# Six buffers for blocks of x in place of two, with room from the q/k loads and from v, and another order of the last layers

## The chip, the core and the metric

One core of a Trainium2 chip runs the whole program. The metric is the device time of one execution in microseconds (us); lower is better.

Engines are named as in the profile: PE (TensorE, matrix products; PEld its weight loads), DVE (VectorE), ACT (ScalarE), POOL (GpSimd) and SP (SyncE, which issues nearly all DMAs here). Each takes its own instructions in the order written and stands still when the next one waits.

## What is computed

Attention with the 32 largest scores of each row, and behind it a two-layer network on its output.

```python
# q, k, v: (B, H, S, D) = (8, 8, 576, 64)
scores = matmul(q, k.transpose(0, 1, 3, 2)) / sqrt(D)
kth = np.partition(scores, -32, axis=-1)[..., -32:-31]
scores = np.where(scores >= kth, scores, -1e9)
attn = softmax(scores)
x = matmul(attn, v).transpose(0, 2, 1, 3).reshape(4608, 512)
h = x @ w_in                                  # (4608, 2048)
out = (h / (1 + exp(-1.702 * h))) @ w_out     # (4608, 512)
```

## The kernel before, in words

**Slots.** The attention is cut into 144 slots, 18 in each of the 8 batches. A slot holds 128 rows of scores for the two heads of a pair (there are four pairs, `hp` 0 to 3). Of the 576 rows of a batch, four blocks `t` of 128 give 16 slots; the 64 rows left over go, for two pairs at once, into 2 slots, which stand ahead of the last block's four (line 262 on). So a batch's slots are t=0 (four pairs), t=1, t=2, two end slots, t=3.

**Iterations.** Slots 0 to 11 run one by one (`slot`, L754) while the weights come in. From slot 12 on `two_slots(n)` (L836) handles slots n and n+1, n even; one call is called an iteration here. In it DVE finds the largest of slots n and n+1; ACT masks, exponentiates and splits slots n-1 and n into 16-bit halves (`split`, L457), which SP writes to memory (`rows`) and brings back transposed (`turn_by_dma`, L465, tile `pt`, two buffers); PE multiplies slots n-3 and n-2 by v (`values_at`, L517); ACT copies the products (L902); and POOL scales them into x (`x_of`, L535, L544). PE also makes the scores of slots ahead (L281), and two steps of each layer.

**x and the layers.** A block of x, transposed, is a tile `xT` of 128 x 4 x 128 numbers, filled by the four pairs of one t. The 64 rows left over of two batches share a tile `xT_t`. When the last pair is in, `finish_x` (L549) appends the block to the list `ready`. `hidden` (L566) takes the oldest block on that list and makes a quarter of its first layer (16 products, L575) in PSUM tile `ph`. `tanh` (L587, ACT) and `gate` (L599, POOL's L604 and L605, or DVE's L607 in the end) turn that into `th`, and `project` (L612, four products, L622) adds it to the second layer's `po`. Each iteration calls `hidden` twice and `project` twice, so a block takes two iterations in each layer. In 36 slots (two batches) nine blocks become ready, at an uneven pace: the block of the ends comes in the odd batch just ahead of t=3, so that around the change from an odd batch to the next two blocks wait while the next are being filled.

```python
    loads = pool("loads", 2)      # q and k of a pair, as loaded
    vals = pool("vals", 6)        # v of a pair
    xtp = pool("xtp", 2)          # blocks of x
```

**Loads.** A table says in which slot, counted from a batch's first, the steps for the pairs are written into the program (L651 to L655, L670 on): FETCH loads q and k of a pair (`load`, L171: six DMAs into one tile `qk_l`), READY makes halves of it on ACT (`prepare_by_dma`, L234, tile `halves`), writes these to memory (`qk_rows`, four DMAs) and brings them back transposed (`turn`, L250, tile `qk_t`), and VALUES loads v (`load_v`, L195: three DMAs). The names with `_1` are for batch 1, which comes while the weights still arrive. SP thus issues, in one order, loads of q, k and v, `qk_rows`, `qk_t`, `rows`, `pt` and the output. It stands still ahead of a DMA whose source isn't written or whose target isn't free.

**The end.** After slot 143 the loop goes on without attention, and `last_slot` (L828) works off what is left:

```python
    def last_slot():
        tanh(False)
        gate(False)
        if may_project(0):
            project(range(G))
        hidden()
```

Of the kernel before, what the change touches and what calls it, by code (L numbers as in the profile page):

```python
# [9 lines left out]
ALU = mybir.AluOpType  # L10
ENG = mybir.EngineType
F32 = mybir.dt.float32
# [6 lines left out]
P = 128  # L19
# [11 lines left out]
def kernel(  # L31
# [27 lines left out]
    nc = tc.nc  # L59
# [11 lines left out]
    G = 4  # L71
# [17 lines left out]
    const = ctx.enter_context(tc.tile_pool(name="const", bufs=1))  # L89
    pool = lambda name, bufs, **kw: ctx.enter_context(tc.tile_pool(name=name, bufs=bufs, **kw))  # L90
    raws = pool("raws", 8)
    loads = pool("loads", 2)
    vals = pool("vals", 6)
    qkt = pool("qkt", 6)
    scp = pool("scp", 4)
    prp = pool("prp", 2)
    lefts = pool("lefts", 2)
    small = pool("small", 4)
    ptp = pool("ptp", 2)
    xtp = pool("xtp", 2)  # L100
    xtt = pool("xtt", 1)
    thp = pool("thp", 5)
    apart = pool("apart", 4, space=DRAM)
# [54 lines left out]

    qT, kT, vv = {}, {}, {}
    loaded = {}  # L160
    v_ends = [const.tile([P, 2, D], F32, name=f"v_e{i}") for i in range(6)]
    for i, t in enumerate(v_ends):
        (nc.gpsimd if i else nc.vector).memset(t[:], 0.0)

# [6 lines left out]
    def load(name, b, hp, queue=None):  # L171

        src = q if name == "q" else k
        if (b, hp) not in loaded:
            loaded[b, hp] = loads.tile([P, 2 * NF + 1, 2, D], F32, name="qk_l")
        t = loaded[b, hp]
        if queue is None:
            heads_of = lambda j: of_load(name, t)[:, :, j, :]
        else:
            heads_of = lambda j: heads_apart(name, t)[:, j, :, :]  # L180
        queue = queue or nc.sync
        for j in range(2):
            queue.dma_start(heads_of(j), src[b, 2 * hp + j, 0:FULL, :].rearrange("(p t) d -> p t d", t=NF))

        on = slice(0, TAIL) if name == "q" else slice(TAIL, P)
        queue.dma_start(t[on, 2 * NF, :, :], src[b, 2 * hp : 2 * hp + 2, FULL:S, :].rearrange("h p d -> p h d"))
# [283 lines left out]

    xts = {}

    def values(n, put_off=None):

        b, t, hps = slots[n]
        pt = st[n]["pt"]
        outs = []
        for p in range(2 if t == NF else 1):
            cols = slice(p * TAIL, (p + 1) * TAIL) if t == NF else slice(0, P)
            main, tail = vv[b, hps[p]]  # L480
            o = ps_t.tile([P, 512], F32, name="o", tag="tp")
            for c in range(NF + 1):
                for j in range(2):
                    nc.tensor.matmul(
                        o[j * D : (j + 1) * D, 0 : cols.stop - cols.start],
                        lhsT=main[:, j, c, :] if c < NF else tail[:, j, :],
                        rhs=pt[:, MAIN[j] + c if c < NF else NF, cols],
                        start=(c == 0),
                        stop=(c == NF),
                    )  # L490
            outs.append((o, hps[p]))
        st[n].clear()

        def bring():
            for o, hp in outs:
                if t < NF:
                    if (b, t) not in xts:
                        xts[b, t] = xtp.tile([P, CC, P], F32, name="xT")
                    nc.scalar.copy(out=xts[b, t][:, hp, :], in_=o[:, 0:P])
                else:  # L500
                    if (b // 2, t) not in xts:
                        xts[b // 2, t] = xtt.tile([P, CC, P], F32, name="xT_t")
                    at = b % 2 * TAIL
                    nc.scalar.copy(out=xts[b // 2, t][:, hp, at : at + TAIL], in_=o[:, 0:TAIL])
            finish_x(n)

        if put_off is None:
            bring()
        else:
            put_off.append(bring)  # L510
# [24 lines left out]
    def x_of(m, o, by):  # L535

        b, t, hps = slots[m]
        for p in range(2 if t == NF else 1):
            cols = slice(p * TAIL, (p + 1) * TAIL) if t == NF else slice(0, P)
            key, tile_of = ((b // 2, t), xtt) if t == NF else ((b, t), xtp)  # L540
            if key not in xts:
                xts[key] = tile_of.tile([P, CC, P], F32, name="xT_t" if t == NF else "xT")
            to = slice(b % 2 * TAIL, (b % 2 + 1) * TAIL) if t == NF else cols
            nc.gpsimd.tensor_tensor(  # L544
                out=xts[key][:, hps[p], to], in0=o[:, cols], in1=by[:, cols], op=ALU.mult
            )
        finish_x(m)

    def finish_x(m):  # L549

        b, t, hps = slots[m]
        if hps[-1] == NP - 1:
            if t < NF:
                to = out[b * S : b * S + FULL, :].rearrange("(p t) c -> p t c", t=NF)[:, t, :]
                ready.append((xts.pop((b, t)), [(slice(0, P), to)]))
            elif b % 2:
                first = [(b - 1 + i) * S + FULL for i in range(2)]
                rows = [(slice(i * TAIL, (i + 1) * TAIL), out[x : x + TAIL, :]) for i, x in enumerate(first)]
                ready.append((xts.pop((b // 2, t)), rows))

    ready = []
    hidden_at = {"g": 0}
    to_gate, gated, to_project = [], [], []
    proj = {}

    def hidden(into=None):  # L566
        if not ready:
            return
        xT, rows = ready[0]
        g = hidden_at["g"]  # L570
        ph = (into or ps_h).tile([P, G, P], F32, name="ph", tag="tp" if into else "ph")
        for i in range(G):
            f = g * G + i
            for c in range(CC):
                nc.tensor.matmul(  # L575
                    ph[:, i, :],
                    lhsT=win[:, c, f * P : (f + 1) * P],
                    rhs=xT[:, c, :],
                    start=(c == 0),
                    stop=(c == CC - 1),  # L580
                )
        to_gate.append((ph, g, rows))
        hidden_at["g"] = (g + 1) % NG
        if g == NG - 1:
            ready.pop(0)

    def tanh(aside):  # L587

        if to_gate:
            ph, g, rows = to_gate.pop(0)  # L590
            th = thp.tile([P, G, P], F32, name="th")
            nc.scalar.activation(th[:], ph[:], AF.Tanh, scale=0.851 / RAISE)  # L592
            if aside:
                h = raws.tile([P, G, P], F32, name="h", tag="raw")
                nc.scalar.copy(out=h[:], in_=ph[:])
                ph = h
            gated.append((th, ph, g, rows))

    def gate(aside):  # L599
        if not gated:  # L600
            return
        th, h, g, rows = gated.pop(0)
        if aside:
            nc.gpsimd.tensor_scalar(th[:], th[:], 1.0, 1.0, op0=ALU.add, op1=ALU.mult)  # L604
            nc.gpsimd.tensor_tensor(out=th[:], in0=th[:], in1=h[:], op=ALU.mult)  # L605
        else:
            nc.vector.scalar_tensor_tensor(  # L607
                out=th[:], in0=th[:], scalar=1.0, in1=h[:], op0=ALU.add, op1=ALU.mult
            )
        to_project.append((th, g, rows))  # L610

    def project(blocks, put_off_leaving=False):  # L612

        if blocks[0] == 0:
            proj["on"] = to_project.pop(0)
            if proj["on"][1] == 0:
                proj["po"] = ps_p.tile([P, C], F32, name="po")
        gT, g, rows = proj["on"]
        po = proj["po"]
        for i in blocks:  # L620
            f = g * G + i
            nc.tensor.matmul(  # L622
                po[:], lhsT=gT[:, i, :], rhs=wout[:, f, :], start=(f == 0), stop=(f == FC - 1)
            )
        if blocks[-1] == G - 1 and g == NG - 1:
            def leave():
                ob = thp.tile([P, C], F32, name="ob", tag="th")
                nc.scalar.mul(out=ob[:], in_=po[:], mul=0.5 / RAISE**2)
                for on, to in rows:
                    nc.sync.dma_start(to, ob[on, :])  # L630

            leaving.append(leave)
            if not put_off_leaving:
                leave_all()

# [13 lines left out]


    READY = (-12, -10, -4, -2)  # L651
    READY_1 = (-6, -4, -3, -2)
    FETCH = (-16, -14, -8, -6)
    FETCH_1 = (-12, -10, -5, -3)
    VALUES = (-2, -1, 1, 2)  # L655
    by_slot = dict(enumerate([2, 2, 3, 3, 3, 3, 3, 3, 3, 3, 2, 2]))
    for n in by_slot:
        first = sum(map(len, list(by_slot.values())[:n]))
# [21 lines left out]

    def may_project(waiting):

        return len(to_project) > waiting and len(finished) >= NG * CC + (to_project[0][1] + 1) * G

    def both_heads(to, src, t):

# [67 lines left out]
    def slot(n):  # L754
# [65 lines left out]
            for fn, args in preparing:  # L820
                fn(*args)
        if n > PROJECTS and may_project(2):
            project(range(G))
        if idle:
            stay_warm(8)
        hidden()
# [1 line left out]
    def last_slot():  # L828

        tanh(False)  # L830
        gate(False)
        if may_project(0):
            project(range(G))
        hidden()

    def two_slots(n):  # L836

# [21 lines left out]

        def project_one():  # L860
            if may_project(0):
                project(range(G), True)

        def measure(m):
            if live(m):
# [90 lines left out]
```

## Time and profile before

| | |
|---|---|
| time, median of 3 runs | 1560.32 us (1559.6 to 1564.83) |
| the profiled execution | 1561.79 us, its span 1560.0 us |
| mean granted clock of TensorE, share of full speed | 0.972 |
| busy share PE, PEld, DVE, ACT, POOL | 94%, 68%, 88%, 75%, 57% |
| chain that ended last, by engine | PE 26%, DVE 3%, ACT 2%, POOL 1% |

The span runs from the first to the last instruction of the profile; the execution's time has a little around it. An idle stretch of an engine is put down to what ended it ("<-"). Products in 32-bit numbers show as two MATMUL records each, so that a quarter of the first layer counts x32 and one of the second x8. The sequencer of SP is called SPq; the us of a row of it are the time of issuing, not of the transfer.

### The profile page before, as it was taken

To read this page: it belongs to the slowest core of one execution; us is meant where nothing else is said; L and a number is where in the kernel's file an instruction comes from. 1 tells how busy PE (TensorE), PEld (TensorE's weight loads), DVE (VectorE), ACT (ScalarE), POOL (GpSimd) and SP (SyncE) were. 2 spreads that over 40 slices of the span, in tenths; PEclk is the share of its full clock that TensorE was granted. 3 is DMA by queue.
4 is the path that set the end of the run, shared out by engine and by line. 5 is a ranking of instruction groups with operands and counts; after the bars stand their busy time and mean duration, and the time that the engine had idled before them with its cause. 6 is when DMAs were issued, how large, how long until landed. Compare 5 with 4: busy or idle time off the path is not lost. (4 is left out here: it accounts for less than half of the span.)

```text
span 1560.0 us, 31382 instructions
## 1 busy us (share of the span) xinstructions
PE 1461.0 (94%) x10729; PEld 1059.6 (68%) x10729; DVE 1375.2 (88%) x4542; ACT 1171.5 (75%) x1846; POOL 888.9 (57%) x1119
## 2 busy tenths in 40 slices
PE   7789789999999899999998899999998899999997
PEld 5667556777766577777776577777775677777765
DVE  7999989999989799999997799999997889999700
ACT  6998778888768687878786687888876688777710
POOL 3788555666645566666665466666664566666400
PEclk8899899999999999999999999999999999999999
DMA  7451786767755486677767576676765658444500
GB/s 241 134 160 36 194 214 184 194 172 183 189 156 162 126 199 173 173 176 181 187 162 161 128 186 190 163 189 175 179 172 146 161 147 203 131 128 130 145 23 14
DMA packets 533778, 248.35 MB, mean 159 GB/s; under 512 B 465136, under 2 KB 507889, under 8 KB 533617
## 3 DMA queue, kind: packets, MB, share of 16 engines
q1 hardware_dynamic: 533184, 246.05, 60.3%
q8 instruction: 84, 1.38, 0.4%
q14 instruction: 78, 0.63, 0.1%
q10 hardware_dynamic: 432, 0.30, 0.1%
HBM read 45.09 MB, written 105.32 MB: 96 GB/s over the span
## 5 line engine op out<-in xcount | busy, mean ns | idle before, releaser
L622 PE MATMUL po<-wout,th 128*128 128x512 f32 x1152 | 534.2, 608 | 43.9 <-POOL th L605 35.4
L575 PEld LDWEIGHTS ph<-xT,win 128*128 128x128 f32 x4096 | 473.9, 192 | 69.6 <-issue 53.2
L575 PE MATMUL ph<-xT,win 128*128 128x128 f32 x4096 | 489.3, 277 | 12.3 <-POOL xT L544 12.3
L622 PEld LDWEIGHTS po<-wout,th 128*128 128x128 f32 x1152 | 213.5, 195 | 264.5 <-issue 216.4
L336 DVE MAX8 top<-left 128x8 f32<-128x288 f32 x792 | 325.3, 445 | 0.0
L461 ACT COPY sc<-pr 128x2304 uint16<-128x2304 uint16 x133 | 281.5, 2117 | 2.2
L293 ACT ACTIVATE sc<-s_ps 128x576 f32<-128x576 f32 x288 | 172.2, 654 | 140.6 <-PE s_ps L281 130.3
L544 POOL TENSOR_TENSOR xT<-x 128x128 f32<-128x128 f32 x117 | 51.7, 458 | 392.6 <-DVE top L343 215.1
L390 ACT ACTIVATE pr<-sc,low 128x576 f32<-128x576 f32 x288 | 220.6, 774 | 47.7 <-POOL low L367 47.7
L336 DVE MAX8 top<-lesser 128x8 f32<-128x288 f32 x528 | 214.1, 446 | 37.1 <-POOL lesser L326 37.1
L339 DVE MATCH_REPLACE8 left<-top,left 128x288 f32<-128x288 f32 x528 | 229.6, 442 | 0.0
L387 ACT ACTIVATE sc<-sc,cut 128x576 f32<-128x576 f32 x288 | 208.7, 783 | 2.7 <-POOL cut L378 2.1
L326 POOL TENSOR_TENSOR lesser<-lesser,greater 128x576 int32<-128x576 int32 x132 | 186.0, 1409 | 22.7 <-DVE greater L322 13.2
L325 POOL TENSOR_TENSOR lesser<-sc 128x576 int32<-128x576 int32 x132 | 187.6, 1421 | 0.0
L281 PE MATMUL s_ps<-qk_t 64*128 64x288 f32 (+1 forms) x1280 | 185.2, 436 | 1.0 <-ACT sc L293 0.8
L605 POOL TENSOR_TENSOR th<-th,h 128x512 f32<-128x512 f32 x127 | 161.9, 1275 | 10.6
L526 PE MATMUL o<-pt,v_l 128*64 128x128 f32 (+1 forms) x2384 | 147.5, 268 | 11.0 <-DMA pt<-rows 11.0
L526 PEld LDWEIGHTS o<-pt,v_l 128*64 128x64 f32 x2384 | 122.7, 139 | 38.1 <-issue 22.9
L592 ACT ACTIVATE th<-ph 128x512 f32<-128x512 f32 x144 | 86.6, 602 | 81.0 <-PE ph L575 80.9
L322 DVE TENSOR_TENSOR greater<-sc 128x576 f32<-128x576 f32 x132 | 104.6, 792 | 44.7 <-ACT sc L293 35.4
L281 PEld LDWEIGHTS s_ps<-qk_t 64*128 64x128 f32 (+1 forms) x1280 | 100.8, 180 | 42.6 <-issue 22.1
L339 DVE MATCH_REPLACE8 left<-top,greater 128x288 f32<-128x288 f32 x264 | 114.8, 442 | 0.0
(86 smaller groups left out, 1606.2 us busy)
## 6 DMA issues: line engine op xcount, KB each, us to landing
rows<-sc SPq DMA_DIRECT2D x133, 576.0 KB, 3.1
qk_rows<-halves SPq DMA_DIRECT2D x56, 256.0 KB, 2.8
qk_l<-in_q_dram SPq DMA_DIRECT2D x64, 128.0 KB, 3.0
raw<-in_moe_w_in_dram SPq DMA_DIRECT2D x16, 512.0 KB, 5.2
v_l<-in_v_dram SPq DMA_DIRECT2D x32, 256.0 KB, 3.2
raw<-in_moe_w_out_dram SPq DMA_DIRECT2D x16, 512.0 KB, 3.6
out_dram<-ob SPq DMA_DIRECT2D x32, 256.0 KB, 2.9
qk_l<-in_k_dram SPq DMA_DIRECT2D x62, 128.0 KB, 2.9
```

What stands on the lines that cost most here:

```text
L281: nc.tensor.matmul(ps[i][rows, c, 0:HALF], lhsT=qT[b, hps[p]][on, cols], rhs=kT[b, hps[p]][on, FIRST[i] + c * HALF : FIRST[i] + (c + 1) * ...
L293: nc.scalar.mul(out=to, in_=ps[i][:, :, 0:HALF], mul=SCALE)
L325: nc.gpsimd.tensor_tensor(out=whole, in0=a.bitcast(I32), in1=b.bitcast(I32), op=ALU.add)
L326: nc.gpsimd.tensor_tensor(out=whole, in0=whole, in1=greater[n][:].bitcast(I32), op=ALU.subtract)
L336: nc.vector.max(top[:, i, 8 * r : 8 * r + 8], src[:, i, :])
L339: nc.vector.match_replace(to[:, i, :], top[:, i, 8 * r : 8 * r + 8], src[:, i, :], LOWEST)
L387: nc.scalar.activation(sc[:, i, :], sc[:, i, :], AF.Prelu, bias=cut[:, i : i + 1], alpha=HUGE)
L390: nc.scalar.activation(pr[:, i * S : (i + 1) * S], sc[:, i, :], AF.Exp, bias=low[:, i : i + 1], accum_out=den[:, i : i + 1],)
L461: nc.scalar.copy(out=halves, in_=pr[:].bitcast(U16).rearrange("p (k h) -> p h k", h=2))
L526: nc.tensor.matmul(o[j * D : (j + 1) * D, cols], lhsT=main[:, j, c, :] if c < NF else tail[:, j, :], rhs=pt[:, MAIN[j] + c if c < NF else ...
L575: nc.tensor.matmul(ph[:, i, :], lhsT=win[:, c, f * P : (f + 1) * P], rhs=xT[:, c, :], start=(c == 0), stop=(c == CC - 1),)
L622: nc.tensor.matmul(po[:], lhsT=gT[:, i, :], rhs=wout[:, f, :], start=(f == 0), stop=(f == FC - 1))
```

## The change

It has five parts.

1. `xtp` has three tiles, each with room for two blocks (t=0 and 1, or t=2 and 3), so six blocks in place of two. A tile comes free when both its blocks are read.
2. `loads` has one buffer in place of two; in batch 0 pairs 1 and 3 are loaded into the two buffers of `pt`, which are not yet in use.
3. `vals` has four buffers in place of six, and the zeroed tiles for the ends of v (`v_e`) are four in place of six.
4. The table is moved: loads of q and k come later, for a pair often right behind the preparation of the pair ahead of it, and loads of v later by up to one slot.
5. `last_slot` calls `hidden` ahead of `gate` and `project`, and takes PSUM buffers of `ps_t` for every other quarter.

`hidden` and `project` are also written for several blocks at once; each entry on `ready` still holds one block, and they make the same products.

```diff
-    loads = pool("loads", 2)
-    vals = pool("vals", 6)
+    loads = pool("loads", 1)
+    vals = pool("vals", 4)
...
-    xtp = pool("xtp", 2)
+    xtp = pool("xtp", 3)
...
-    v_ends = [const.tile([P, 2, D], F32, name=f"v_e{i}") for i in range(6)]
+    v_ends = [const.tile([P, 2, D], F32, name=f"v_e{i}") for i in range(NP)]
...
-            loaded[b, hp] = loads.tile([P, 2 * NF + 1, 2, D], F32, name="qk_l")
+            home, tag = (ptp, "pt") if b == 0 and hp % 2 else (loads, "qk_l")
+            loaded[b, hp] = home.tile([P, 2 * NF + 1, 2, D], F32, name="qk_l", tag=tag)
...
+    def x_at(b, t, hp):
+
+        if t < NF:
+            if (b, t // 2) not in xts:
+                xts[b, t // 2] = xtp.tile([P, CC, 2, P], F32, name="xT")
+            return xts[b, t // 2][:, hp, t % 2, :]
+        if b // 2 not in xts:
+            xts[b // 2] = xtt.tile([P, CC, P], F32, name="xT_t")
+        return xts[b // 2][:, hp, b % 2 * TAIL : (b % 2 + 1) * TAIL]
...
-            nc.gpsimd.tensor_tensor(
-                out=xts[key][:, hps[p], to], in0=o[:, cols], in1=by[:, cols], op=ALU.mult
-            )
+            nc.gpsimd.tensor_tensor(out=x_at(b, t, hps[p]), in0=o[:, cols], in1=by[:, cols], op=ALU.mult)
...
-    READY_1 = (-6, -4, -3, -2)
-    FETCH = (-16, -14, -8, -6)
-    FETCH_1 = (-12, -10, -5, -3)
-    VALUES = (-2, -1, 1, 2)
+    READY_1 = (-7, -4, -3, -2)
+    FETCH = (-16, -11, -8, -3)
+    FETCH_1 = (-12, -6, -3, -2)
+    VALUES = (-1, 1, 1, 3)
...
     def last_slot():
 
         tanh(False)
+        hidden(ps_t if hidden_at["f"] % (2 * G) else None)
         gate(False)
         if may_project(0):
-            project(range(G))
-        hidden()
+            project()
```

READY = (-12, -10, -4, -2) stays. On PE, POOL and DVE nothing else moves than what stands in the last fences here and two `memset` of POOL's at the start.

SP's queue in the iteration of slots 50 and 51 (slot -4 of batch 3), before: `qk_t` of pair 2, then `rows` and `pt` of slot 50, then v of pair 0.

```order
L469 DMA_TRANSPOSE pt<-rows 128x9x256
L252 DMA_TRANSPOSE qk_t<-qk_rows 128x2432
L463 DMA rows<-sc 128x2304
L469 DMA_TRANSPOSE pt<-rows 128x9x256
L197 DMA v_l<-in_v_dram 128x2x256
L205 DMA v_e_117<-in_v_dram 64x64 x2
```

The same place now:

```order
L470 DMA_TRANSPOSE pt<-rows 128x9x256
L253 DMA_TRANSPOSE qk_t<-qk_rows 128x2432
L184 DMA qk_l<-in_q_dram 128x4x64 x2
L187 DMA qk_l<-in_q_dram 64x2x64
L184 DMA qk_l<-in_k_dram 128x4x64 x2
L187 DMA qk_l<-in_k_dram 64x2x64
L464 DMA rows<-sc 128x2304
L470 DMA_TRANSPOSE pt<-rows 128x9x256
```

The six DMAs of pair 3's q and k, which stood two slots earlier, now stand between `qk_t` and the `rows` of slot 50. The same holds at slot -12 of a batch for pair 1: twice for each of the batches 2 to 7, so at twelve places.

SP's queue where batch 1 is prepared (slots 11 to 13), before:

```order
L463 DMA rows<-sc 128x2304
L243 DMA qk_rows<-halves 128x4x256 x2
L247 DMA qk_rows<-halves 128x256
L248 DMA qk_rows<-halves 64x256
L630 DMA out_dram<-ob 128x512
L469 DMA_TRANSPOSE pt<-rows 128x9x256
L252 DMA_TRANSPOSE qk_t<-qk_rows 128x2432
L183 DMA qk_l<-in_q_dram 128x4x64 x2
L186 DMA qk_l<-in_q_dram 64x2x64
L183 DMA qk_l<-in_k_dram 128x4x64 x2
L186 DMA qk_l<-in_k_dram 64x2x64
L463 DMA rows<-sc 128x2304
```

The same place now:

```order
L244 DMA qk_rows<-halves 128x4x256 x2
L248 DMA qk_rows<-halves 128x256
L249 DMA qk_rows<-halves 64x256
L184 DMA qk_l<-in_q_dram 128x4x64 x2
L187 DMA qk_l<-in_q_dram 64x2x64
L184 DMA qk_l<-in_k_dram 128x4x64 x2
L187 DMA qk_l<-in_k_dram 64x2x64
L464 DMA rows<-sc 128x2304
L636 DMA out_dram<-ob 128x512
L470 DMA_TRANSPOSE pt<-rows 128x9x256
L253 DMA_TRANSPOSE qk_t<-qk_rows 128x2432
L464 DMA rows<-sc 128x2304
```

Here `qk_rows` of pair 0 and a load of six DMAs stand ahead of the first `rows`, and no load between the first `qk_t` and the second `rows`.

PE's last instructions, before:

```order
L575 MATMUL ph<-xT_t,win 128x128 x16
L622 MATMUL po<-wout,th 128x512 x8
L575 MATMUL ph<-xT_t,win 128x128 x16
L622 MATMUL po<-wout,th 128x512 x4
L575 MATMUL ph<-xT,win 128x128 x16
L622 MATMUL po<-wout,th 128x512 x4
L575 MATMUL ph<-xT,win 128x128 x16
L622 MATMUL po<-wout,th 128x512 x4
L575 MATMUL ph<-xT,win 128x128 x16
L622 MATMUL po<-wout,th 128x512 x4
L575 MATMUL ph<-xT,win 128x128 x16
L622 MATMUL po<-wout,th 128x512 x4
```

And now:

```order
L580 MATMUL ph<-xT_t,win 128x128 x16
L628 MATMUL po<-wout,th 128x512 x4
L580 MATMUL ph<-xT_t,win 128x128 x16
L628 MATMUL po<-wout,th 128x512 x4
L580 MATMUL ph<-xT,win 128x128 x16
L628 MATMUL po<-wout,th 128x512 x4
L580 MATMUL ph<-xT,win 128x128 x16
L628 MATMUL po<-wout,th 128x512 x4
L580 MATMUL ph<-xT,win 128x128 x16
L628 MATMUL po<-wout,th 128x512 x4
L580 MATMUL ph<-xT,win 128x128 x16
L628 MATMUL po<-wout,th 128x512 x8
```

The count of products is the same; each quarter of the second layer now stands behind the first layer of the quarter after its own, and the last two stand together.

## Rows read from the trace of the kernel before

**Rows 1.** Busy time in two stretches of 39 us; columns as in its head.
```profile
core 0: us, PE busy (x) PEld busy (x) DVE busy (x) ACT busy (x) POOL busy (x), PEclk, DMA share, GB/s
507.00:546.00 39.00, 33.18 (x251) 23.38 (x252) 29.07 (x100) 24.65 (x37) 23.06 (x29) 0.91 0.45 126
741.00:780.00 39.00, 39.00 (x285) 28.21 (x281) 38.22 (x133) 30.49 (x50) 24.23 (x31) 1.00 0.73 187
```

**Rows 2.** Who waited for whom, whole span: us in total, times, longest us.
```profile
PE po L622 <- POOL th L605: 35.4, 7, 5.8
PE ph L575 <- POOL xT L544: 12.3, 16, 1.1
PE o L526 <- DMA pt<-rows: 11.0, 3, 6.0
PE po L622 <- DVE th L607: 7.0, 5, 1.4
...
POOL xT L544 <- PE ph L575: 55.4, 6, 9.2
```

**Rows 3.** Timeline of POOL, the writes of x alone: start us, us, instruction, idle before.
```profile
435.35 0.88 POOL L544 TENSOR_TENSOR xT<-x 128x128 f32<-128x128 f32 x2 [6.37 <-DVE top L343]
...
454.54 0.46 POOL L544 TENSOR_TENSOR xT<-x 128x128 f32<-128x128 f32 x1 [4.90 <-ACT x L902]
464.21 0.45 POOL L544 TENSOR_TENSOR xT<-x 128x128 f32<-128x128 f32 x1 [9.21 <-PE ph L575]
...
481.52 0.87 POOL L544 TENSOR_TENSOR xT<-x 128x128 f32<-128x128 f32 x2 [6.01 <-DVE top L343]
...
500.61 0.46 POOL L544 TENSOR_TENSOR xT<-x 128x128 f32<-128x128 f32 x1 [4.80 <-ACT x L902]
...
528.46 0.88 POOL L544 TENSOR_TENSOR xT<-x 128x128 f32<-128x128 f32 x2 [6.87 <-DVE top L343]
```

**Rows 4.** Timeline of PE, second layer in an iteration of each kind.
```profile
444.86 3.60 PE L622 MATMUL po<-wout,th 128*128 128x512 f32 x8
...
469.94 5.58 PE L622 MATMUL po<-wout,th 128*128 128x512 f32 x8 [5.82 <-POOL th L605]
```

**Rows 5.** Timeline of PE in the end, with and without waits.
```profile
1490.11 3.60 PE L622 MATMUL po<-wout,th 128*128 128x512 f32 x8
1493.55 3.73 PE L575 MATMUL ph<-xT_t,win 128*128 128x128 f32 x32
1497.12 3.60 PE L622 MATMUL po<-wout,th 128*128 128x512 f32 x8
...
1543.73 3.70 PE L622 MATMUL po<-wout,th 128*128 128x512 f32 x8 [1.41 <-DVE th L607]
1547.27 3.73 PE L575 MATMUL ph<-xT,win 128*128 128x128 f32 x32
1552.41 3.70 PE L622 MATMUL po<-wout,th 128*128 128x512 f32 x8 [1.41 <-DVE th L607]
```

**Rows 6.** Timeline of SP's queue around slot 50.
```profile
549.14 2.38 SPq L252 DMA_TRANSPOSE qk_t<-qk_rows  x1
551.61 0.54 SPq L463 DMA_DIRECT2D rows<-sc  x1
555.10 2.37 SPq L469 DMA_TRANSPOSE pt<-rows  x1
```

**Rows 7.** Timeline of PE: slot 50 times v, one iteration later.
```profile
563.28 1.05 PE L526 MATMUL o<-pt,v_l 128*64 128x128 f32 x16
```

**Rows 8.** Timeline of SP's queue at the start: a load between `qk_t` and `rows`.
```profile
162.87 2.43 SPq L252 DMA_TRANSPOSE qk_t<-qk_rows  x1
165.35 1.26 SPq L183 DMA_DIRECT2D qk_l<-in_q_dram  x2
...
169.38 0.54 SPq L463 DMA_DIRECT2D rows<-sc  x1
173.05 2.63 SPq L469 DMA_TRANSPOSE pt<-rows  x1
```

**Rows 9.** Timeline of PE there.
```profile
177.73 1.12 PE L526 MATMUL o<-pt,v_l 128*64 128x64 f32 x16 [4.70 <-DMA pt<-rows]
```

**Rows 10.** DMA issues: kind, count, median us to landing.
```profile
pt<-rows SPq DMA_TRANSPOSE x133, 4.8
```

More of the change, by code (lines that the diff above doesn't have):

```diff
@@ L495, in bring @@
             for o, hp in outs:
[L496 to L504, printed above, removed]
+                to = x_at(b, t, hp)
+                nc.scalar.copy(out=to, in_=o[:, 0 : to.shape[-1]])
             finish_x(n)
@@ L539, in x_of @@
             cols = slice(p * TAIL, (p + 1) * TAIL) if t == NF else slice(0, P)
[L540 to L543, printed above, removed]
-            nc.gpsimd.tensor_tensor(
-                out=xts[key][:, hps[p], to], in0=o[:, cols], in1=by[:, cols], op=ALU.mult
-            )
+            nc.gpsimd.tensor_tensor(out=x_at(b, t, hps[p]), in0=o[:, cols], in1=by[:, cols], op=ALU.mult)
         finish_x(m)
@@ L551, in finish_x @@
         b, t, hps = slots[m]
[L552 to L556, printed above, removed]
+        if hps[-1] < NP - 1:
+            return
+        if t == NF:
+            if b % 2:
                 first = [(b - 1 + i) * S + FULL for i in range(2)]
                 rows = [(slice(i * TAIL, (i + 1) * TAIL), out[x : x + TAIL, :]) for i, x in enumerate(first)]
-                ready.append((xts.pop((b // 2, t)), rows))
+                xT = xts.pop(b // 2)
+                ready.append(([xT[:, c, :] for c in range(CC)], [rows]))
+            return
+        lines = out[b * S : b * S + FULL, :].rearrange("(p t) c -> p t c", t=NF)
+        xT = xts[b, t // 2]
+        ready.append(([xT[:, c, t % 2, :] for c in range(CC)], [[(slice(0, P), lines[:, t, :])]]))
+        if t % 2:
+            del xts[b, t // 2]
     ready = []
-    hidden_at = {"g": 0}
+    hidden_at = {"f": 0}
     to_gate, gated, to_project = [], [], []
-    proj = {}
+    pos = []
     def hidden(into=None):
@@ L569, in hidden @@
         xT, rows = ready[0]
[L570 to L573, printed above, removed]
+        tiles = len(rows)
+        f0 = hidden_at["f"]
+        fs = range(f0, f0 + G // tiles)
+        ph = (into or ps_h).tile([P, G * P], F32, name="ph", tag="tp" if into else "ph")
+        for i, f in enumerate(fs):
             for c in range(CC):
                 nc.tensor.matmul(
-                    ph[:, i, :],
+                    ph[:, i * tiles * P : (i + 1) * tiles * P],
                     lhsT=win[:, c, f * P : (f + 1) * P],
-                    rhs=xT[:, c, :],
+                    rhs=xT[c],
                     start=(c == 0),
@@ L581, in hidden @@
                 )
-        to_gate.append((ph, g, rows))
-        hidden_at["g"] = (g + 1) % NG
-        if g == NG - 1:
+        to_gate.append((ph, fs, rows))
+        hidden_at["f"] = fs.stop % FC
+        if fs.stop == FC:
             ready.pop(0)
@@ L590, in tanh @@
             ph, g, rows = to_gate.pop(0)
-            th = thp.tile([P, G, P], F32, name="th")
+            th = thp.tile([P, G * P], F32, name="th")
             nc.scalar.activation(th[:], ph[:], AF.Tanh, scale=0.851 / RAISE)
             if aside:
-                h = raws.tile([P, G, P], F32, name="h", tag="raw")
+                h = raws.tile([P, G * P], F32, name="h", tag="raw")
                 nc.scalar.copy(out=h[:], in_=ph[:])
@@ L610, in gate, with project, leave @@
         to_project.append((th, g, rows))
[L612 to L626, printed above, removed]
+    def project(put_off_leaving=False):
+        gT, fs, rows = to_project.pop(0)
+        if fs.start == 0:
+            pos[:] = [
+                home.tile([P, C], F32, name="po", tag=tag) for home, tag in ((ps_p, "po"), (ps_h, "ph"))[: len(rows)]
+            ]
+        blocks = iter(range(G))
+        for f in fs:
+            for po in pos:
+                i = next(blocks)
+                nc.tensor.matmul(
+                    po[:], lhsT=gT[:, i * P : (i + 1) * P], rhs=wout[:, f, :], start=(f == 0), stop=(f == FC - 1)
+                )
+        if fs.stop == FC:
+            def leave(po, to_rows):
                 ob = thp.tile([P, C], F32, name="ob", tag="th")
                 nc.scalar.mul(out=ob[:], in_=po[:], mul=0.5 / RAISE**2)
-                for on, to in rows:
+                for on, to in to_rows:
                     nc.sync.dma_start(to, ob[on, :])
-            leaving.append(leave)
+            leaving.extend(lambda po=po, to=to: leave(po, to) for po, to in zip(pos, rows))
             if not put_off_leaving:
@@ L681, in may_project @@
     def may_project(waiting):
-        return len(to_project) > waiting and len(finished) >= NG * CC + (to_project[0][1] + 1) * G
+        return len(to_project) > waiting and len(finished) >= NG * CC + to_project[0][1].stop
     def both_heads(to, src, t):
@@ L830, in last_slot @@
         tanh(False)
+        hidden(ps_t if hidden_at["f"] % (2 * G) else None)
         gate(False)
         if may_project(0):
-            project(range(G))
-        hidden()
+            project()
     def two_slots(n):
@@ L861, in project_one @@
             if may_project(0):
-                project(range(G), True)
+                project(True)
         def measure(m):
```

## The prediction

> **What bounds the kernel now.** I read the table by stretches first, since busy shares of the whole span mix stages. In an undisturbed stretch PE is busy all of the time and DVE 38.22 of 39 us, at granted clock 1.00 [rows 1]: two full engines, PE the fuller. In the stretch from 507 us PE has 33.18 us, DVE 29.07, and the mean clock is 0.91 of 2.4 GHz. So the kernel runs at PE's pace except in some stretches, and the question is what stops it there.
>
> The waits of the whole span answer it. POOL waits six times, 55.4 us in all, to write x until PE has read the block whose buffer it needs; on PE the second layer waits for POOL's gate 35.4 us in seven waits of up to 5.8 us [rows 2]. The timeline of POOL's writes of x shows both ends of that: at 454.54 the first write of an iteration, then 9.21 us of idle until the second, for which PE's first layer had to end; the same again from 500.61 [rows 3]. POOL takes its work in order, so the sums DVE needs and the gate of the second layer stand behind the write that waits; PE finds no gate and idles 5.82 us, and its next eight products take 5.58 us where they else take 3.60 [rows 4]. PE idles because POOL waits for PE, a loop that a spare buffer cuts.
>
> Six waits are two at each of three places: where an odd batch ends and the next begins, three such changes ahead of the last batch. That fits the order of the work: there two finished blocks lie in wait (ends and t=3) while t=1 and then t=2 of the next batch begin, and with two buffers each beginning must wait.
>
> **Part 1, six buffers.** The price of a place is read from the starts of successive iterations [rows 3]. Undisturbed: 454.54 - 435.35 = 19.2 and 500.61 - 481.52 = 19.1 us. With a wait: 481.52 - 454.54 = 27.0 and 528.46 - 500.61 = 27.9 us. Over 19.1 that is 7.9 + 8.7 = 16.6 us; three places give 49.9. As a cross-check from PE's side, the idle 5.82 and the slow products' 1.98 make 7.8 for the first [rows 4]. The 9.21 us of POOL's wait itself is no price: part of it lies beside PE's work.
>
> All of it is gained if PE can hold 19.1 there. It does so right before and between the two waits, with the same products per iteration (its order does not change there), so I take the full 49.9. What is late next is PE itself at 19.1, DVE closely behind. Three tiles of two blocks are enough: at most two finished blocks wait, one is read, one is filled, and a tile is asked for again only six blocks later. The sixteen short waits of PE for a block just finished, 12.3 us [rows 2], stay: PE's order is the same, and there no buffer is missing.
>
> **Part 5, the end.** Before, PE alternates eight records of `po` with the next first layer and waits 1.41 us ahead of each for tanh and gate of what it has just made. The period is 1552.41 - 1543.73 = 8.68 us; where other work fills the wait it is 1497.12 - 1490.11 = 7.01 [rows 5]. The waits are five [rows 2], so 5 x 1.67 = 8.4 us. Now another quarter of the first layer, 3.73 us, lies between a quarter's first layer and its second, more than the 1.41; and the last gate runs under the last but one `po`, 3.70. So I take all 8.4; the bound on the other side is 0. The buffers asked for are free: every other quarter goes to the two of `ps_t`, which the attention has left.
>
> A page speaks against this part. The Trainium skill (TensorE: Matmul & The Clock Gate, section on HAM oscillation) tells of a kernel in which a second PSUM buffer for the products gave nothing more. By that the sum would be 8.4 us higher; here no run shows it yet, and the rows show the wait.
>
> **Parts 2 and 4, what it costs.** All of it falls on SP's queue. Pair 3's load now stands between `qk_t` and the `rows` of slot 50. Before, `qk_t` was issued by 549.14 + 2.38 = 551.52, `rows` at 551.61 and `pt` at 555.10 [rows 6]. The only places of this trace with a load there are at the start: from the load's first DMA to `rows` 169.38 - 165.35 = 4.03 us, from `rows` to `pt` 3.67 [rows 8]. With these, `rows` of slot 50 goes at 551.6 + 4.0 = 555.6 and `pt` at 559.3; it lands 4.8 us later [rows 10], at 564.1. PE wants it at 563.28 [rows 7]. So PE waits 0.8 us where it had 3.4 to spare. There are twelve such places. Six lie in iterations of 19.1 us, as this; in the other six PE comes about a us later, by its wait for a fresh block, and I take nothing. That is 6 x 0.8 = 4.8 us. Bounds: 0, and all of the load exposed everywhere, 12 x 4.03 = 48.
>
> At the start, two of PE's waits for `pt` are 11.0 us less a trifle, up to 6.0 each [rows 2]; the first, 4.70, follows just such a load [rows 9], and now the load stands ahead of it, while later loads of pairs 2 and 3 stand closer before their use on ACT. The first wait may go (-4.7) or another of the longest kind come (+6.0). I take 0.
>
> The rest I cost at nothing. Loads of v come up to a slot later, with more than an iteration until their use; they may now wait for PE to have read the old v, but in SP's order they stand behind a `pt` that had to wait for PE's products of the slot ahead in any case. If that cover fails, the price is again a late `rows`. Pairs 1 and 3 of batch 0 lie in `pt`'s buffers, which are asked for only slots later. Two `memset` of POOL's fall away at the start, beside loads.
>
> **The sum.** 1560.0 - 49.9 - 8.4 + 4.8 + 0 = 1506.5 us of span; the execution has 1.8 more around it, and the median of the runs lies 1.5 below that execution, so **1507 us**. A change of 0.3%, 5 us, is about the least a measurement of this kernel tells from none.
>
> **Rivals.**
>
> *SP runs late.* If half of the 4.03 us is exposed at all twelve places, 24 in place of 4.8: 1526. For it: 0.8 us past the mark leaves no slack for a slower transfer. Against: behind each place SP has an iteration with no load. Chance 0.13.
>
> *Slower.* The gain of 58.3 is lost when each of the twelve costs over 58.3/12 = 4.9 us. That takes more than the load: with one buffer, it can't be issued before ACT has made the halves of the pair ahead, and `rows`, `pt` and `qk_t` of all that follows stand behind it, so that the next iteration is late too. At PE's longest wait for `pt`, 6.0 us, it makes 12 x 6.0 = 72, less 58: 1574. Against: the halves are long done at these places, since `qk_rows`, ahead in the queue, wants them too. Chance 0.03. The Trainium skill (DMA: Bandwidth & Descriptors, section on the anatomy of one DMA) says that a wait is made by the issuing sequencer before it hands the DMA on, so that one wait holds all behind it; that is the rule this rival needs.
>
> *It doesn't do what it says.* A tile of two blocks is held until both are read; if that makes three tiles too few, the six waits stay and only the end is gained: 1560 - 8.4 + 4.8 = 1557. Against: the count above. Chance 0.04.
>
> *The end gives nothing*, by the page above or since PE's products there were stretched over the wait: 1507 + 8 = 1515. Chance 0.05.
>
> *More.* The sixteen waits of 12.3 us go as well, as POOL is never behind: 1495. Against: PE's order puts the first layer right behind the write. Chance 0.06.
>
> **How the numbers follow.** The forecast has 0.69, and by its own bounds (SP's term 0 to 10, the start -4.7 to +6) runs from 1498 to 1518. To leave out no more than 2 in 10 the range takes in the dearer end, the cheaper half of "more" and the nearer half of "SP late": 1495 to 1523. Faster: 0.69 + 0.13 + 0.05 + 0.06 = 0.93; the third rival is within 5 us, 0.04; slower 0.03.
>
> **What would show it.** In the new profile the wait of POOL's x for PE's first layer is gone; POOL's writes of x come 19.1 to 20.2 us apart all the way; PE's wait for POOL's gate shrinks to a us or so, and the granted clock is 1.00 between 430 and 1440 us. In the end PE has no wait for DVE's gate. PE's wait for `pt` grows, in twelve small pieces at most, and shows the SP term. The forecast is wrong if intervals over 21 us remain after the start, and the reading of the cause is wrong if POOL's wait is gone and the time isn't.

## The result, and the profile after

| | before | after |
|---|---|---|
| median of the runs shown together | 1561.67 us (4 runs) | 1513.07 us (1511.96 to 1513.73, 4 runs) |
| the profiled execution, its span | 1561.79 us, 1560.0 us | 1512.53 us, 1510.7 us |
| mean granted clock of TensorE, share of full speed | 0.972 | 0.983 |

The ratio of the times, after over before, is 0.9686, with a 95% interval of 0.9667 to 0.9706. (Every ratio below is against the kernel before, measured beside it.) By the spans the gain is 49.3 us, where the sum said 53.5 (1560.0 to 1506.5). The time lies in the range, 6 us above the 1507. Of these, 4.2 us lie between the spans, nearly all in one place, the start. The other 2 come from taking the median of the runs 1.5 us below the profiled execution, as it was before; here it lies 0.5 above.

The table by stretches, with the windows of [rows 1]:

```profile
core 0: us, PE busy (x) PEld busy (x) DVE busy (x) ACT busy (x) POOL busy (x), PEclk, DMA share, GB/s
507.00:546.00 39.00, 39.00 (x300) 28.38 (x299) 38.06 (x131) 32.14 (x50) 24.67 (x32) 1.00 0.60 160
741.00:780.00 39.00, 39.00 (x280) 28.17 (x280) 38.19 (x131) 30.35 (x49) 24.64 (x32) 1.00 0.72 178
```

The stretch from 507 us, which had 33.18 us of PE at clock 0.91, is now like the undisturbed one. From 430 to 1440 us the mean clock is 1.00, as forecast; before it was 0.98 there. PE's waits over the whole span (us in total, times, longest), to be held against [rows 2]:

```profile
PE ph L580 <- POOL xT L544: 12.0, 16, 0.9
PE o L530 <- DMA pt<-rows: 10.4, 7, 3.6
PE s_ps L282 <- ACT sc L294: 9.1, 2, 8.4
...
PE tp L217 <- DMA qk_l<-in_q_dram: 3.6, 1, 3.6
```

The waits for POOL's gate (35.4 us) and for DVE's (7.0) are gone from the list, and so is POOL's wait for the first layer (55.4). What is new stands in the third and the last line: a wait for ACT's scores of up to 8.4 us, where before there was one of 0.8, and one of 3.6 us for q where before it was 1.2 us. The writes of x, POOL's timeline, at the place of [rows 3]:

```profile
440.22 0.87 POOL L544 TENSOR_TENSOR xT<-x 128x128 f32<-128x128 f32 x2 [6.38 <-ACT x L908]
459.40 0.87 POOL L544 TENSOR_TENSOR xT<-x 128x128 f32<-128x128 f32 x2 [4.90 <-ACT x L908]
478.43 0.87 POOL L544 TENSOR_TENSOR xT<-x 128x128 f32<-128x128 f32 x2 [6.29 <-DVE top L344]
497.52 0.87 POOL L544 TENSOR_TENSOR xT<-x 128x128 f32<-128x128 f32 x2 [4.80 <-DVE top L344]
516.56 0.87 POOL L544 TENSOR_TENSOR xT<-x 128x128 f32<-128x128 f32 x2 [6.30 <-ACT x L908]
```

They come 19.0 to 19.2 us apart, and both writes of an iteration stand together; nothing parts them for 9.21 us any more. The second layer at the place of [rows 4] takes its 3.60 us:

```profile
465.27 3.73 PE L580 MATMUL ph<-xT,win 128*128 128x128 f32 x32
468.84 3.60 PE L628 MATMUL po<-wout,th 128*128 128x512 f32 x8
```

The end, PE's timeline, to be held against [rows 5]: the period is 1492.77 - 1485.77 = 7.00 us, no wait.

```profile
1485.77 3.60 PE L628 MATMUL po<-wout,th 128*128 128x512 f32 x8
1489.20 3.73 PE L580 MATMUL ph<-xT,win 128*128 128x128 f32 x32
1492.77 3.60 PE L628 MATMUL po<-wout,th 128*128 128x512 f32 x8
1496.21 3.73 PE L580 MATMUL ph<-xT,win 128*128 128x128 f32 x32
1499.78 7.03 PE L628 MATMUL po<-wout,th 128*128 128x512 f32 x16
```

To find where the time went I laid the two traces side by side by one row that comes once per iteration, PE's `o<-ident,wide`, and took the difference of the intervals. Here are the row near 313 us and the ends of the first long interval, before:

```profile
312.48 0.38 PE L515 MATMUL o<-ident,wide 128*128 128x128 f32 x2
...
448.29 0.38 PE L515 MATMUL o<-ident,wide 128*128 128x128 f32 x2
...
475.36 0.38 PE L515 MATMUL o<-ident,wide 128*128 128x128 f32 x2
```

And after:

```profile
317.36 0.38 PE L519 MATMUL o<-ident,wide 128*128 128x128 f32 x2
...
453.17 0.38 PE L519 MATMUL o<-ident,wide 128*128 128x128 f32 x2
...
472.27 0.38 PE L519 MATMUL o<-ident,wide 128*128 128x128 f32 x2
```

Six intervals are shorter, by 8.0, 8.8, 8.2, 8.9, 8.2 and 8.9: **51.0 us** (forecast 49.9). From the last of these rows to PE's last product, 55.55 us became 47.18: **8.4** (forecast 8.4). Four later intervals are longer, by 0.45, 1.41, 3.07 and 0.29: **5.2** (forecast 4.8). And ahead of 320 us the new kernel is **4.9** behind (forecast 0). 51.0 + 8.4 - 5.2 - 4.9 = 49.3.

One of the longer intervals, from 898.60 us, now takes 22.2 us. The prediction named an interval over 21 us behind the start as a sign that it is wrong, so by its own sign it failed at this one place. What the interval holds is PE's wait for `pt` and not POOL's wait for PE.

### The profile page after: what moved, and what is told of

Read it like the earlier page. It is cut to its first block, busy times and chain, and to the rows that moved or that the text cites. A ratio compares the mean times of both kernels' runs of the same rounds, so it can differ in the third digit from the quotient of the medians.

```text
span 1510.7 us, 31439 instructions
## 1 busy us (share of the span) xinstructions
PE 1443.9 (96%) x10729; PEld 1052.8 (70%) x10729; DVE 1378.1 (91%) x4542; ACT 1171.7 (78%) x1846; POOL 891.1 (59%) x1117
## 5 line engine op out<-in xcount | busy, mean ns | idle before, releaser
L628 PE MATMUL po<-wout,th 128*128 128x512 f32 x1152 | 518.5, 593 | 1.5 <-POOL wout L147 1.5
L628 PEld LDWEIGHTS po<-wout,th 128*128 128x128 f32 x1152 | 208.1, 191 | 211.1 <-issue 207.9
L327 POOL TENSOR_TENSOR lesser<-lesser,greater 128x576 int32<-128x576 int32 x132 | 186.0, 1409 | 22.2 <-DVE greater L323 12.7
L530 PE MATMUL o<-pt,v_l 128*64 128x128 f32 (+1 forms) x2384 | 146.2, 266 | 10.5 <-DMA pt<-rows 10.4
L609 POOL TENSOR_SCALAR th<-th 128x512 f32<-128x512 f32 x127 | 78.8, 620 | 66.2 <-ACT th L597 66.0
```

Of the source, the lines that this page charges most:

```text
L327: nc.gpsimd.tensor_tensor(out=whole, in0=whole, in1=greater[n][:].bitcast(I32), op=ALU.subtract)
L530: nc.tensor.matmul(o[j * D : (j + 1) * D, cols], lhsT=main[:, j, c, :] if c < NF else tail[:, j, :], rhs=pt[:, MAIN[j] + c if c < NF else ...
L628: nc.tensor.matmul(po[:], lhsT=gT[:, i * P : (i + 1) * P], rhs=wout[:, f, :], start=(f == 0), stop=(f == FC - 1))
```

## The experiments

**1. The end alone.** The kernel before, with:

```diff
         tanh(False)
+        hidden(ps_t if hidden_at["g"] % 2 else None)
         gate(False)
         if may_project(0):
             project(range(G))
-        hidden()
```

> The kernel before with the new order of the last layers alone. Theory (the two gains add, the end is worth 8.4 us by itself): span 1560.0 - 8.4 = 1551.6 us, no wait of PE for DVE's gate in the end, POOL's six waits for the first layer as before, 55 us. Rival (the end gives nothing without the rest): span 1560.

Measured: ratio 0.9955 (0.9942 to 0.9969), span 1553.0. POOL's waits stay:

```profile
POOL xT L544 <- PE ph L575: 55.3, 6, 9.2
```

and from the last `o<-ident,wide` to the end it takes 47.18 us, as in the changed kernel. The end is worth its 8.4 us by itself; the span is 1.4 longer than expected since this run was 2.9 behind by 320 us, in code that is the same as before, while its six long intervals were 1.6 shorter in sum. The new order and the extra PSUM buffers came together; which of the two the gain needs was not tried.

**2. Three single blocks.** The kernel before, with:

```diff
-    vals = pool("vals", 6)
+    vals = pool("vals", 5)
...
-    xtp = pool("xtp", 2)
+    xtp = pool("xtp", 3)
```

> The kernel before with three buffers for single blocks of x (one buffer of v gives the room), loads and end as before. Theory A (one spare block cuts the loop; in the changed kernel's trace no more than three blocks seem to be in use at once): all six waits go, 51.0 us as the change gained in its six iterations, and neither the 4.9 us at the start nor the 5.2 us of waits for pt come: span 1509.0 us. Theory B (the prediction's count: two blocks wait, one is read, one is filled, so four are needed): the second wait of each of the three places stays, 8.8 us each: span about 1535. If the 10 us of the start and of pt came from the blocks and not from the loads, span 1519.

Measured: ratio 0.9678 (0.9665 to 0.9691), span 1509.2. POOL's wait for the first layer is gone from the list, the six intervals are 19.0 to 19.1 us, and no later interval is longer than before. Theory A: one spare block, 2 KB of each partition, gives all 51 us. My count of four was wrong.

**3. Three single blocks and the end.** Both edits above.

> Three single blocks and the new order of the last layers, loads as before. Theory A: 1560.0 - 51.0 - 8.4 = span 1500.6 us, time about 1502.4, ten below the change. Theory B (three blocks too few): about 1527. If the loads' new places cost nothing (the 10 us come from elsewhere): 1510.7, as the change.

Measured: ratio 0.9629 (0.9616 to 0.9642), median 1503.13, span 1501.2. The gains add, and without moved loads the kernel is 9.5 us of span below the change. PE waits for `pt` twice, both times in the start, and never behind it:

```profile
177.09 1.12 PE L526 MATMUL o<-pt,v_l 128*64 128x64 f32 x16 [3.94 <-DMA pt<-rows]
225.45 1.98 PE L526 MATMUL o<-pt,v_l 128*64 128x128 f32 x16 [7.18 <-DMA pt<-rows]
```

**4. Two tiles of two blocks.** The change, with:

```diff
-    xtp = pool("xtp", 3)
+    xtp = pool("xtp", 2)
```

> The change with two tiles of two blocks in place of three. Theory A (the count of blocks alone matters, three are enough, four are there): as the change, span 1510.7 us. Rival (a tile comes free only when both its blocks are read): t=0 and 1 of an even batch find a free tile, t=2 must wait for t=3 of the odd batch, so one wait of some 9 us stays at each of the three places, costing 8.8 us each: span 1537.

Measured: span 1510.9, median 1511.95, ratio 0.9687 (0.9674 to 0.97), as the change. Theory A again: that a tile is held until both blocks are read costs nothing here. A third of the room that the change gives to x isn't needed.

**5. The late loads alone.** Experiment 3, with:

```diff
-    FETCH = (-16, -14, -8, -6)
+    FETCH = (-16, -11, -8, -3)
```

> Three single blocks, new end, two load buffers as before, and only the changed kernel's table for loads of q and k of batches 2 to 7. Theory A (the place in SP's queue costs it: the load stands ahead of rows and pt): PE's waits for pt come back in odd batches, some 5.2 us together, span 1501.2 + 5.2 = 1506.4 us. Rival (the single buffer costs it): no such wait, span 1501.2.

Measured: median 1507.75 (ratio 0.9665, 0.9643 to 0.9687), 4.6 above experiment 3. The profiled execution is the fastest of four, with span 1502.4: it was 3.1 ahead of experiment 3's trace by 320 us, and lost 4.4 to it behind that. The waits for `pt` are back, behind 500 us:

```profile
564.47 1.09 PE L526 MATMUL o<-pt,v_l 128*64 128x128 f32 x16 [0.99 <-DMA pt<-rows]
817.65 1.09 PE L526 MATMUL o<-pt,v_l 128*64 128x128 f32 x16 [0.39 <-DMA pt<-rows]
913.84 1.09 PE L526 MATMUL o<-pt,v_l 128*64 128x128 f32 x16 [0.30 <-DMA pt<-rows]
1263.48 1.09 PE L526 MATMUL o<-pt,v_l 128*64 128x128 f32 x16 [1.24 <-DMA pt<-rows]
```

With two buffers for the loads this can't be the single one: it is the place in SP's queue. Theory A, and at the same four places, those of the odd batches, though at three of them one iteration later than in the changed kernel, and with other sizes. The four waits make 2.9 of the 4.4 us.

**6. The new table for batch 1 alone.** Experiment 3, with:

```diff
-    READY_1 = (-6, -4, -3, -2)
+    READY_1 = (-7, -4, -3, -2)
...
-    FETCH_1 = (-12, -10, -5, -3)
+    FETCH_1 = (-12, -6, -3, -2)
```

> Three single blocks, new end, two load buffers, and only the changed kernel's table for batch 1 (loads and preparation). Theory A (the place of the loads of pairs 2 and 3, close ahead of their use, costs it): ACT waits some 6 and 5 us for the halves' source, PE some 8 us for ACT's scores, and the kernel is behind by 4.9 us from then on, less the 0.6 that three blocks alone lose there: span about 1505.5 us. Rival (the single buffer costs it): no such waits, 1501.2.

Measured: median 1503.70 (ratio 0.9631, 0.9616 to 0.9645), span 1502.3. Neither theory. The waits came as theory A said, in ACT and in PE:

```profile
ACT halves L239 <- DMA qk_l<-in_k_dram: 11.8, 2, 7.1
```
```profile
PE s_ps L281 <- ACT sc L293: 10.2, 2, 9.5
...
PE o L526 <- DMA pt<-rows: 2.2, 2, 1.7
```

but they cost 1.1 us of span and not 4.3, since PE's waits for `pt` fall from 11.1 to 2.2 us: with the loads out of `pt`'s way one wait takes the place of another. So most of the 4.9 us came from elsewhere, and I went further back in the trace.

**7. Which pairs lie in `pt`'s buffers.** At the very start, in SP's queue of the changed kernel, the load of pair 2 is held:

```profile
6.66 1.07 SPq L126 DMA_DIRECT2D raw<-in_moe_w_in_dram  x2
13.01 1.24 SPq L184 DMA_DIRECT2D qk_l<-in_q_dram  x2
```

What SP waits for there:

```profile
SPq L184 <- PE tp L694: 5.2, 1, 5.2
```

Line 694 is the last reading of pair 0, which ends at 12.97. Before, the load went at 11.16, and SP waited 2.4 us for line 220, the last reading of pair 1: of two buffers the load took the one that came free first. Now it has only pair 0's. PE then waits for it:

```profile
16.56 1.08 PE L217 MATMUL tp<-ident,qk_l 128*128 128x128 f32 x4 [3.59 <-DMA qk_l<-in_q_dram]
...
170.96 0.44 PE L519 MATMUL o<-ident,wide 128*128 128x128 f32 x2 [2.90 <-POOL wide L425]
```

The second row is the first of the iterations; before it stood at 168.80. The experiment is the change, with:

```diff
-            home, tag = (ptp, "pt") if b == 0 and hp % 2 else (loads, "qk_l")
+            home, tag = (ptp, "pt") if b == 0 and hp % 2 == 0 else (loads, "qk_l")
```

> The change with pairs 0 and 2 of batch 0 in pt's two buffers (and 1 and 3 in the loads' one) in place of pairs 1 and 3. Theory (at the very start SP holds the load of pair 2 until PE has read pair 0 for the last time, at 13.0 us where before it was 11.2, and all of the start is 2.2 us later from there on): that wait goes, PE's wait of 3.6 us for q at 16.6 us shrinks to 1.2 or less, the first slot's sums come at 168.8 us or earlier in place of 171.0, span 1508.5. Rival (the 2.2 us are chance, as the start differs by a us or two from kernel to kernel): no shift, 1510.7.

Measured: median 1508.42 (1506.06 to 1509.46; ratio 0.9652, 0.9639 to 0.9665), 4.6 below the change; span 1507.7, 3.0 below it. The load goes at 7.77, and:

```profile
14.01 0.63 PE L217 MATMUL tp<-ident,qk_l 128*128 128x128 f32 x4 [0.52 <-DMA qk_l<-in_q_dram]
...
168.50 0.44 PE L519 MATMUL o<-ident,wide 128*128 128x128 f32 x2 [2.88 <-POOL wide L425]
```

The theory holds: by this pair of traces 2.5 us of the start are this one buffer. The size is not firmer than that. In the seven traces with the loads of batch 0 as before, the first `o<-ident,wide` stands anywhere from 166.44 to 169.66; in the two with the change's (the change and experiment 4) it stands at 170.96 and 171.92.

**8. The steps swapped.** This one goes after the sixteen waits that are left. Experiment 3, with, in the second half of `two_slots`:

```diff
+        project_one()
         hidden(ps_t)
         if live(n + 3):
             copy_scores(n + 3)
         tanh(aside)
         prepare_some(second)
-        project_one()
```

> Three single blocks, new end, and in each iteration the second step of the second layer ahead of the second step of the first layer on PE, so that a block just finished has 3.6 us more. Theory (the sixteen waits for a fresh block only need time; iterations of 20.1 us become 19.1): 16 x 1.0 = 16.0 us gained, span 1485.2. Rival (tanh and gate of the step that now ends the iteration come too late for the second layer of the next one): a wait of PE for POOL's gate in most of some 60 iterations, half a us or more each, span 1531 or more.

Measured: median 1490.36 (ratio 0.9544, 0.953 to 0.9559), span 1488.8, 12.4 below experiment 3. Iterations that took 20.1 us take 19.0 to 19.2, and of PE's waits for POOL's x and gate these are left:

```profile
PE po L622 <- POOL th L605: 2.2, 2, 1.8
...
PE ph L575 <- POOL xT L544: 1.2, 1, 1.2
```

The theory holds up to the last iterations: there, once attention thins out, the gate comes 1.84 us too late one time. That, and a start that differs, is why 12.4 us came and not the 16.0 expected; fifteen of the intervals are 15.1 us shorter in sum. The rival's wait in every iteration didn't come.

**9. Swapped, and batch 0 in four buffers.** Experiment 8, with:

```diff
-            loaded[b, hp] = loads.tile([P, 2 * NF + 1, 2, D], F32, name="qk_l")
+            home, tag = (ptp, "pt") if b == 0 and hp > 1 else (loads, "qk_l")
+            loaded[b, hp] = home.tile([P, 2 * NF + 1, 2, D], F32, name="qk_l", tag=tag)
```

> The swapped steps, three single blocks and the new end, and pairs 2 and 3 of batch 0 in pt's two buffers, so that no load of batch 0 waits for a buffer. Theory: the loads of pair 2 go 2 us sooner, the span falls below 1488.8 by what PE waits there for q and k, 1 to 2 us, to about 1487. Rival (the weights set the pace of the start, and the loads are hidden or come in their way): 1488.8 or a little more.

Measured: median 1488.90 (1487.45 to 1490.17), ratio 0.953 (0.9517 to 0.9543), span 1487.3; its first `o<-ident,wide` stands at 167.69, in experiment 8 at 168.35. By the traces it is 1.5 us better than experiment 8; by the times alone the two can't be told apart, as their intervals overlap. The load of pair 2 did go sooner, at 7.79 us and not at 10.59, but PE had its q no sooner: its product starts at 14.16, after a wait of 1.36, where in experiment 8 it started at 14.14. That speaks for the rival, and the 1.5 us are not shown to come from the loads. The median is the lowest here, 24 us below the change.

## Why the prediction was right, and where it was off

**The loop of PE and POOL** was read rightly: 49.9 forecast, 51.0 measured, and experiment 2 gets it by one more block alone. The price came from the intervals between POOL's writes [rows 3], not from POOL's wait of 55.4 us, and came nearer. The count behind "three tiles of two blocks are enough" was too careful: four blocks, two finished, one read and one filled, are never all needed at once, and three are enough (experiment 2).

**The end** gave its 8.4 us, alone (experiment 1) and with the rest, so the rival that it gives nothing falls.

**SP's term** has the right size, 5.2 for 4.8, and experiment 5 shows the cause: the place of the load in the queue. That the two sums meet so closely is partly luck, as its inner working was off. I had 0.8 us at each of six places; what came, at places among these six, was three waits of PE for `pt`, 0.23, 1.19 and 2.84 us, in intervals that are 0.45, 1.41 and 3.07 longer, and a fourth interval, longer by 0.29, in which no such wait is listed:

```profile
551.79 1.09 PE L530 MATMUL o<-pt,v_l 128*64 128x128 f32 x16 [0.23 <-DMA pt<-rows]
824.76 1.09 PE L530 MATMUL o<-pt,v_l 128*64 128x128 f32 x16 [1.19 <-DMA pt<-rows]
```

In the traces of experiments 4, 5 and 7 the longer intervals of the loop make 5.6, 4.4 and 6.0 us, in other pieces. The load itself took its 4.0 us at all twelve places (4.0 to 4.9 in the changed kernel's rows of SP), so the 3.4 us of slack are used up, or nearly so, everywhere. What decides then is how fast `rows` lands. From `rows` to `pt` I took 3.67 [rows 8]; the median of 96 such gaps behind 300 us is 3.4, and the dearest place is this one:

```profile
887.84 2.38 SPq L253 DMA_TRANSPOSE qk_t<-qk_rows  x1
890.27 1.26 SPq L184 DMA_DIRECT2D qk_l<-in_q_dram  x2
...
894.30 0.54 SPq L464 DMA_DIRECT2D rows<-sc  x1
899.73 2.33 SPq L470 DMA_TRANSPOSE pt<-rows  x1
```
```profile
904.31 1.09 PE L530 MATMUL o<-pt,v_l 128*64 128x128 f32 x16 [2.84 <-DMA pt<-rows]
```

with a gap of 5.43 us. That is 1.8 over the 3.67 that I took, and with the 0.8 that I had worked out it makes 2.6 of the 2.84. It isn't the chance of one execution: in the traces of experiments 4 and 7 the gap at this place is 5.22 and 4.86 us and PE waits 2.15 and 1.98; in experiment 5, with the load at the same place in the queue, the gap is 3.29. Why `rows` lands late just there stays open; the single buffer for loads and the later loads of v, which experiment 5 leaves out, may have a part in it, and neither was tried alone. I said that PE's wait for `pt` grows; in total it fell from 11.0 to 10.4. In the start three waits of 11.0 us became four of 6.1, while the loop gained 4.3.

**The start** is the term that was mis-sized: 0, with bounds -4.7 to +6.0, measured +4.9. Two steps failed. "Pairs 1 and 3 of batch 0 lie in `pt`'s buffers, which are asked for only slots later" looked at who wants `pt`, and not at which buffer is left for pair 2; that costs 2.2 to 2.5 us by the traces (experiment 7). And in batch 1 the trade that I balanced at zero, one wait for `pt` gone against loads closer to ACT, comes out a little on the dear side. From the first `o<-ident,wide` to the eighth, near 313 us, the four kernels with the new table take 145.0 to 146.4 us, the five with the old one (the swapped ones left out) 143.5 to 145.7. So it is 1.2 us on the mean, 2.7 in the pair of traces that I compared; the two groups overlap, and how much of it is chance isn't settled.

**The rivals.** "SP late" (24 us) and "slower" did not come: at no place in the loop did more than 3.1 us go. "It doesn't do what it says" fell, by experiment 4 even for two tiles. "More" did not come by itself: the sixteen waits stayed at 12.0 us, as argued from PE's order, and it took another order (experiment 8) to be rid of them.

## What to carry to other kernels

Where two engines wait for each other in a loop, price it by the interval between iterations, and count how many buffers are in use at once before making room for more: here one of 2 KB did the work of four, and the room for the others was paid for with loads that came late. When a pool shrinks, list for each tile which buffer it now gets and who read that last, in the first microseconds as well. A wait for a value just made was met here both times, in the end and in experiment 8, by another order of the same work.

## What the runs showed of the hardware that I had not expected

Issuing alone has a price: the six DMAs of a load held SP's queue for 4.0 to 4.9 us at each of the twelve places in the changed kernel, and the `rows` behind them went only then.

Executions of one kernel scatter more than the traces of its loop suggest. Four executions of experiment 5 took 1504.26 to 1512.25 us, five of experiment 3, which differs by two numbers in the table of loads, 1502.71 to 1504.16. In the loop the traces agree to 0.02 us in most iterations. That the late loads cause the scatter is not shown: the change, with its loads at the same places, took 1511.96 to 1513.73, and the kernel before, with none of them in the loop, 1559.60 to 1564.83. Only one execution of each kernel was traced, so what was late in the long ones isn't known.
